# Attention masks: added on VectorE in one fused add and max, and as one strided product per transposed score bank

## The chip, the cores and the metric

The kernel runs on one core of one Trainium2 chip. The metric is the device time of one execution in microseconds (us); the kernel before the change has a median of 1923.84 us over 3 runs (1919.12 to 1926.26). The engines are TensorE (PE, with its weight loads shown apart as PEld), VectorE (DVE), ScalarE (ACT), GpSimd (POOL) and the queue that issues all transfers here, SyncE (SP).

## The reference

One sequence of 2048 rows and 576 columns goes through a sliding-window attention and a mixer with an MLP, each inside an adaptive layer norm. The change touches the attention alone. In short:

```
qkv   = h @ wqkv                       # 32 heads of width 18
scores[h,q,k] = (q . k) * 18**-0.5
mask  = (q - k >= 0) & (q - k < 256)   # each row sees itself and the 255 rows ahead of it
p     = softmax(where(mask, scores, -1e9))
x     = x + ga * ((p @ v) @ wo)
```

Everything else (layer norms, conditioning vector, token mixing, MLP with a GELU) is the same in both kernels.

## The kernel before, in words

The program has four stages, one after the other, with small overlaps: the query/key/value products (to about 228 us of the profile), the attention (to about 735 us), the mixing, and the MLP (from about 1000 us to the end). Each step of a stage is recorded with a due time; the records are sorted by it and written out in that order, so every engine's queue holds its instructions in the order of these times, and nothing is reordered afterwards. The due times of the attention are written as multiples of a head; the change leaves all of them as they are.

The attention goes over 32 units called heads in the code (`n`). A unit holds 512 query rows and two real heads (`j` = 0, 1); units 0 to 7 hold the first 512 rows, where nothing precedes the first row. In each, the scores are computed twice:

- **Row maxima.** Queries stand in blocks of 64 rows. `mx(n, j, bb)` (L440) computes for two blocks a score tile of 128 partitions (64 queries of two real heads) by 320 keys in PSUM, one matmul a block (L448), and then adds the mask with a second matmul, in which the identity is the weight and `Mq` the moving operand (L450, L452). The two PSUM buffers of this tile, `m0` and `m1`, alternate. `red(n, j, bb)` (L454) takes the negated maximum of both blocks in one VectorE reduction (L460), or in two for the narrow blocks of units 0 to 7 (L464). When all eight are there, `mtr` (L466, matmul at L468) transposes the maxima, `mev` copies them on ScalarE, and `mst` sends them by DMA into a row of the query tile, so that the second computation of the scores subtracts them by itself.
- **Transposed scores.** `xm(n, j, k)` (L484) fills five banks of 512 columns with key blocks against query ranges (L492) and adds the masks with one or two identity matmuls a bank (L517). `ex` (L519) takes the exponential of a bank on ScalarE. These banks alternate between `s0` and `s1`.

Every second unit an `av` step (L530) multiplies the exponentials with the values: some 170 to 208 small matmuls in a row on PE. `onm` (L556) normalizes on VectorE. From unit 12 on, every second unit also carries one row tile of the output projection: `otev` (L612) splits the transposed rows, with VectorE at L617 and L618; two runs of 14 matmuls (L629); `woe` (L631) adds each to the residual on VectorE (L633); then come the row statistics (L116 to L118) and the layer norm on VectorE (L642, L643). PE, VectorE and ScalarE each take their instructions strictly in the order of the queue. A buffer is handed on by semaphores: an `mx` matmul cannot start before the reduction two steps earlier has freed its buffer, and `mt` cannot start before the last reduction of its unit.

The loads of a unit are issued on SP behind the maxima of two units earlier.

Of the kernel before, what the change touches and what calls it, by code (L numbers as in the profile page):

```python
# [7 lines left out]
F32 = mybir.dt.float32  # L8
# [3 lines left out]
ALU = mybir.AluOpType  # L12
# [19 lines left out]
class Kern:  # L32
# [8 lines left out]
    def setup(self, stack):  # L41
# [12 lines left out]
        self.rowm = c.tile([P, 8], F32, name="rowm")  # L54
        self.Mq = c.tile([P, 2, 64], F32R, name="Mq")
        self.Mk = c.tile([P, 2, 64], F32R, name="Mk")
        self.md = c.tile([P, 10], F32, name="md")
# [33 lines left out]
    def masks(self):  # L91
        nc = self.nc
        g = nc.gpsimd
        for M in (self.Mq, self.Mk):
            g.memset(M.bitcast(F32), 0.0)
        h = slice(0, 64)
        sel = lambda t, s, op, cm: g.affine_select(out=t, in_=t.bitcast(F32), pattern=[[s, 64]], compare_op=op, fill=NEG, base=0, channel_multiplier=cm)
        sel(self.Mq[h, 0], 1, ALU.is_gt, -1)
        sel(self.Mq[h, 1], -1, ALU.is_ge, 1)
        sel(self.Mk[h, 0], -1, ALU.is_gt, 1)  # L100
        sel(self.Mk[h, 1], 1, ALU.is_ge, -1)
        for M in (self.Mq, self.Mk):
            nc.vector.tensor_copy(M[64:128], M[0:64].bitcast(F32))
        m = self.rowm
# [287 lines left out]
    def attention(self, t1, t2, TA, HU, LX=2.05):  # L392
# [47 lines left out]
        def mx(n, j, bb):  # L440
# [3 lines left out]
            for s in range(2):  # L444
                i = 2 * bb + s
                nb = 5 if g else min(5, i + 1)
                lhs = Q[:, i].rearrange("p r q -> p (r q)")
                nc.tensor.matmul(pm[:, s, 320 - 64 * nb:320], lhs, K[:, j, 64 * (i + 5 - nb):64 * (i + 5)], start=True, stop=False)  # L448
                if nb == 5:
                    nc.tensor.matmul(pm[:, s, 0:320].rearrange("p (a b) -> p a b", b=64)[:, 0::4, :], self.identr, self.Mq, start=False, stop=True)  # L450
                else:
                    nc.tensor.matmul(pm[:, s, 256:320], self.identr, self.Mq[:, 1], start=False, stop=True)  # L452

        def red(n, j, bb):  # L454
# [3 lines left out]
            c = 8 * j + 2 * bb  # L458
            if n >= 8 or bb >= 2:
                nc.vector.tensor_reduce(out=m[:, c:c + 2], in_=pm[:, :, 0:320], axis=mybir.AxisListType.X, op=ALU.max, negate=True)  # L460
# [23 lines left out]
        def xm(n, j, k):  # L484
# [3 lines left out]
            blocks = [x for x in BANKS[k] if g or x[0] >= 0]  # L488
            mk = []
            for i, (b, c) in enumerate(blocks):  # L490
                q0, q1 = rng(b)
                nc.tensor.matmul(px[:, c:c + q1 - q0], K[:, b + 4].rearrange("p r k -> p (r k)"), Q[:, j, q0:q1], start=(i == 0), stop=False)  # L492
                if b >= 0:
                    mk.append((c, 1))
                if b <= 3:
                    mk.append((c + q1 - q0 - 64, 0))
            mk.sort()
            runs = []
            for c, kind in mk:
                if kind == 1 and runs and runs[-1] == (c - 64, 64, 0):  # L500
                    runs[-1] = (c - 64, 128, 0)
                else:
                    runs.append((c, 64, kind))
            if len(runs) == 2 and runs[0][1] == 128 and runs[1][1] == 128:
                d = runs[1][0] - runs[0][0]
                c = runs[0][0]
                out = px[:, c:c + 128]
                o2 = px.rearrange("p (a b) -> p a b", b=64)
                a0, da = c // 64, d // 64
                for h in range(2):  # L510
                    pass
                full = [(o2[:, a0 + h:a0 + h + da + 1:da, :], self.Mk[:, h].unsqueeze(1).to_broadcast([P, 2, 64])) for h in range(2)]
                ops = full
            else:
                ops = [(px[:, c:c + w], self.Mk.rearrange("p a b -> p (a b)")[:, 64 * kind:64 * kind + w]) for c, w, kind in runs]
            for i, (o, mv) in enumerate(ops):
                nc.tensor.matmul(o, self.identr, mv, start=False, stop=(i == len(ops) - 1))  # L517

# [751 lines left out]
```

## Time and profile before

| | |
|---|---|
| median of 3 runs | 1923.84 us (1919.12 to 1926.26) |
| the profiled execution | 1925.45 us, span 1923.7 us |
| mean granted TensorE clock | 0.956 |
| busy, share of the span: PE | 1766.7 us, 92% |
| PEld | 1617.1 us, 84% |
| DVE | 1124.2 us, 58% |
| ACT | 697.9 us, 36% |
| POOL | 899.6 us, 47% |

The page lists, for groups of equal instructions, the line, the engine, the operation, the output and the inputs with their shapes, the count, the busy time, the mean duration in ns, and the idle time just ahead of them with what ended it. A matmul's row gives its duration with the pipeline's length in it; matmuls that follow each other overlap, so a matmul's place in time is read from the distance of two starts. The granted clock is a share of TensorE's full speed.

### The profile page before, as it was taken

What the parts mean: (1) busy time and instruction counts of PE and PEld (TensorE: products, weight loads), DVE (VectorE), ACT (ScalarE), POOL (GpSimd) and SP (SyncE); (2) the same over time, 40 slices, a digit from 0 to 9 for tenths busy, and PEclk for the clock granted to TensorE, in tenths of its full rate; (3) what the DMA queues carried; (4) which work ended last, traced back from release to release, by engine and by line L of the source; (5) the groups of instructions that cost most, each with busy time, mean ns of one, the idle gap of its engine ahead of it and who ended that gap; (6) DMA issues with size and microseconds to landing.
All of it is one profiled execution on the core that took longest, in us unless ns stands there. A gap on an engine that the chain in (4) does not pass through costs nothing.

```text
span 1923.7 us, 34258 instructions
## 1 busy us (share of the span) xinstructions
PE 1766.7 (92%) x13752; PEld 1617.1 (84%) x13752; DVE 1124.2 (58%) x1840; ACT 697.9 (36%) x1194; POOL 899.6 (47%) x831
## 2 busy tenths in 40 slices
PE   7999998989999996787767999999998999999998
PEld 6788888889898986787756999999987899999997
DVE  4544335546665654666646666666676766666664
ACT  2222134434444444423314333333333333333331
POOL 4311364443544444244356556565552555555560
PEclk9999958899999998998887999999998999999999
DMA  4855552443635435444252211121214222222211
GB/s 149 305 178 176 166 144 78 116 123 114 177 110 172 123 93 177 149 154 154 73 175 82 58 58 58 58 58 58 59 56 135 60 58 60 60 61 60 59 46 49
DMA packets 156134, 206.75 MB, mean 107 GB/s; under 512 B 19012, under 2 KB 87620, under 8 KB 155400
## 3 DMA queue, kind: packets, MB, share of 16 engines
q1 hardware_dynamic: 155976, 204.57, 34.6%
q8 instruction: 108, 1.77, 0.4%
q14 instruction: 50, 0.41, 0.1%
HBM read 143.69 MB, written 60.56 MB: 106 GB/s over the span
## 4 chain that ended last, share of the span: by engine, by line
PE 57%; DVE 8%; DMA 3%; POOL 3%; ACT 3%; issue 3%; SPq 1%; DVEq 0%; POOLq 0%; ACTq 0%
PE d L1135 23%; PE av L544 3%; PE wo L629 3%; PE mx L448 2%; PE X L492 2%; PE w L856 2%; PE pg L807 1%; DVE W L994 1%; PE X L517 1%; DVE G L1112 1%; DMA wf<-in_B_w_dram 1%; PE mx L450 1%; PE u33P L1082 1%; PE u32P L1082 1%; PE u26P L1082 1%
## 5 line engine op out<-in xcount | busy, mean ns | idle before, releaser
L1135 PE MATMUL d<-W,G 128*128 128x288 f32 x3456 | 510.2, 298 | 12.5 <-DVE acc L1143 10.0
L1135 PEld LDWEIGHTS d<-W,G 128*128 128x128 f32 x3456 | 490.6, 190 | 35.2 <-DVE acc L1143 10.9
L1143 DVE TENSOR_TENSOR acc<-d,acc 128x576 f32<-128x576 f32 x288 | 216.7, 754 | 193.8 <-PE d L1135 189.5
L974 POOL TENSOR_TENSOR wf<-wf 128x384 f32<-128x384 f32 x140 | 144.9, 1056 | 351.9 <-DMA wf<-in_B_w_dram 351.9
L460 DVE TENSOR_REDUCE m<-mx 128x2 f32<-128x640 f32 x224 | 181.1, 817 | 172.9 <-PE mx L450 171.3
L522 ACT ACTIVATE P<-X 128x512 f32<-128x512 f32 (+4 forms) x320 | 182.0, 573 | 229.1 <-PE X L517 228.0
L448 PE MATMUL mx<-KD,QS 128*128 128x320 f32 (+4 forms) x512 | 168.5, 379 | 28.0 <-POOL QS L431 14.0
L492 PE MATMUL X<-QD,KS 128*128 128x64 f32 (+2 forms) x704 | 156.2, 313 | 1.2 <-ACT P L522 0.7
L431 POOL TENSOR_SCALAR QS<-QD,rowm 128x512 fp32r<-128x512 f32 x128 | 87.8, 699 | 144.0 <-DMA QD<-qd 89.8
L1112 DVE TENSOR_TENSOR G<-U,G 128x512 fp32r<-128x512 f32 x108 | 94.4, 874 | 99.0 <-ACT G L1105 99.0
L986 POOL TENSOR_TENSOR W<-wf,W 128x768 fp32r<-128x768 f32 x70 | 148.8, 2148 | 0.0
L1103 ACT ACTIVATE U<-U 128x512 f32<-128x512 f32 x108 | 68.4, 633 | 189.5 <-DVE U L1088 189.5
L448 PEld LDWEIGHTS mx<-KD,QS 128*128 128x128 f32 x512 | 104.0, 203 | 34.4 <-POOL QS L431 19.3
L1103 ACT ACTIVATE C<-C 128x512 f32<-128x512 f32 x36 | 22.7, 632 | 286.7 <-DVE C L1088 286.7
L278 PE MATMUL qk<-hT,Wqk 128*128 128x512 f32 x504 | 121.3, 402 | 0.0
L278 PEld LDWEIGHTS qk<-hT,Wqk 128*128 128x128 f32 x504 | 96.1, 192 | 24.3 <-issue 0.9
L517 PE MATMUL X<-Mk,identr 128*128 128x128 f32 (+1 forms) x576 | 112.3, 269 | 0.0
L492 PEld LDWEIGHTS X<-QD,KS 128*128 128x128 f32 x704 | 109.1, 199 | 2.5 <-ACT P L522 1.8
L1000 POOL TENSOR_TENSOR wf<-wf,gb 128x1152 f32<-128x1152 f32 x35 | 103.1, 2946 | 13.1 <-DMA wf<-in_B_w_dram 6.9
L438 POOL TENSOR_SCALAR KS<-KD,rowm 128x768 fp32r<-128x768 f32 (+1 forms) x128 | 108.5, 862 | 0.0
L980 ACT CAST W<-wf 128x1152 fp32r<-128x1152 f32 x70 | 90.2, 1319 | 47.2 <-DMA wf<-in_B_w_dram 34.6
L1015 POOL TENSOR_TENSOR W<-wf,W 128x1152 fp32r<-128x1152 f32 x35 | 96.3, 2752 | 13.8 <-ACT W L1009 13.8
(745 smaller groups left out, 3287.2 us busy)
## 6 DMA issues: line engine op xcount, KB each, us to landing
wf<-in_B_w_dram SPq DMA_DIRECT2D x35, 576.0 KB
wf<-in_B_w_dram SPq DMA_DIRECT2D x140, 128.0 KB
KD<-kd SPq DMA_DIRECT2D x72, 216.0 KB
QD<-qd SPq DMA_DIRECT2D x96, 144.0 KB
wf<-in_B_w_dram SPq DMA_DIRECT2D x140, 64.0 KB
qd<-qs SPq DMA_DIRECT2D x16, 512.0 KB
kd<-qs SPq DMA_DIRECT2D x16, 512.0 KB
vd<-Vst SPq DMA_DIRECT2D x16, 312.0 KB
```

What stands on the lines that cost most here:

```text
L278: nc.tensor.matmul(po, W[:, a, fs], H[:, c, :], start=(n == 0), stop=(n == 13))
L438: nc.gpsimd.tensor_scalar(t[:, b0:, r], src[:, b0:], M[:, 2 + r:3 + r], 0.0, op0=ALU.mult, op1=ALU.add)
L448: nc.tensor.matmul(pm[:, s, 320 - 64 * nb:320], lhs, K[:, j, 64 * (i + 5 - nb):64 * (i + 5)], start=True, stop=False)
L460: nc.vector.tensor_reduce(out=m[:, c:c + 2], in_=pm[:, :, 0:320], axis=mybir.AxisListType.X, op=ALU.max, negate=True)
L492: nc.tensor.matmul(px[:, c:c + q1 - q0], K[:, b + 4].rearrange("p r k -> p (r k)"), Q[:, j, q0:q1], start=(i == 0), stop=False)
L517: nc.tensor.matmul(o, self.identr, mv, start=False, stop=(i == len(ops) - 1))
L522: nc.scalar.activation(p[:, lo:], X["px", n, j, k][:, lo:], AF.Exp, scale=SCALE)
L974: nc.gpsimd.tensor_tensor(out=WF[:, o], in0=WF[:, a], in1=WF[:, b], op=ALU.subtract)
L986: eng.tensor_tensor(out=W[:, s0:s1, 3:5, :], in0=WF[:, 1 + s0:1 + s1, 0:2], in1=W[:, s0:s1, 0:2, :].bitcast(F32), op=ALU.subtract)
L1112: nc.vector.tensor_tensor(out=G[:, 1, ta, b], in0=up_b[jj, "gf", ta, b], in1=G[:, 0, ta, b].bitcast(F32), op=ALU.subtract)
L1135: nc.tensor.matmul(po, G[:, g, ta, b, ts], W[:, w, b, cs], start=(n == 0), stop=(n == 5))
L1143: nc.vector.tensor_tensor(out=a, in0=po, in1=a, op=ALU.add)
```

## The change

The mask matmuls of the row maxima go (L450, L452). `Mq` becomes one bf16 row of 320 columns a partition, with the two triangles at both ends and zeros between. `red` issues for each of the two blocks one fused VectorE operation that adds the mask to the scores, writes the sum to a scratch tile `scr` and takes the maximum. The sign that the reduction gave is now given by ScalarE's copy of the transposed maxima, as a multiplication by -1.

In the transposed banks the one or two mask matmuls become one. `Mk` now holds five blocks of 64 columns (two triangles, a zero block, two triangles), and one matmul with 256 moving columns writes to two pieces of 128 columns of the bank, at a stride; where a triangle has no neighbour, the zero block stands beside it. The fifth bank keeps its single matmul.

```diff
-        self.Mq = c.tile([P, 2, 64], F32R, name="Mq")
-        self.Mk = c.tile([P, 2, 64], F32R, name="Mk")
+        self.Mq = c.tile([P, 320], BF16, name="Mq")
+        self.Mk = c.tile([P, 5, 64], F32R, name="Mk")
...
+            X["scr"] = a1([P, 320], F32, name="scr")
...
-                nc.tensor.matmul(pm[:, s, 320 - 64 * nb:320], lhs, K[:, j, 64 * (i + 5 - nb):64 * (i + 5)], start=True, stop=False)
-                if nb == 5:
-                    nc.tensor.matmul(pm[:, s, 0:320].rearrange("p (a b) -> p a b", b=64)[:, 0::4, :], self.identr, self.Mq, start=False, stop=True)
-                else:
-                    nc.tensor.matmul(pm[:, s, 256:320], self.identr, self.Mq[:, 1], start=False, stop=True)
+                nc.tensor.matmul(pm[:, s, 320 - 64 * nb:320], lhs, K[:, j, 64 * (i + 5 - nb):64 * (i + 5)], start=True, stop=True)
...
-            if n >= 8 or bb >= 2:
-                nc.vector.tensor_reduce(out=m[:, c:c + 2], in_=pm[:, :, 0:320], axis=mybir.AxisListType.X, op=ALU.max, negate=True)
-            else:
-                for s in range(2):
-                    w = 64 * (2 * bb + s + 1)
-                    nc.vector.tensor_reduce(out=m[:, c + s:c + s + 1], in_=pm[:, s, 320 - w:320], axis=mybir.AxisListType.X, op=ALU.max, negate=True)
+            for s in range(2):
+                i = 2 * bb + s
+                w = slice(0 if n >= 8 else max(0, 256 - 64 * i), 320)
+                nc.vector.tensor_tensor_reduce(out=X["scr"][:, w], in0=pm[:, s, w], in1=self.Mq[:, w], scale=1.0, scalar=NEG, op0=ALU.add, op1=ALU.max, accum_out=m[:, c + s:c + s + 1])
...
-            nc.scalar.copy(ms, X["mt", n])
+            nc.scalar.mul(ms, X["mt", n], -1.0)
...
+            pairs = lambda c, st: AP(px[:, 0:1].tensor, px[:, c:c + 1].offset, [px[:, 0:1].ap[0], (st, 2), (1, 128)])
+            mk = lambda a, w: self.Mk[:, a:a + w].rearrange("p a b -> p (a b)")
+            split = lambda m: m.rearrange("p (a b) -> p a b", a=2)
+            es = mk(0, 2)
+            both = es.unsqueeze(1).to_broadcast([P, 2, 128])
+            if g:
+                o, mv = ((pairs(0, 256), split(mk(1, 4))), (pairs(128, 256), split(mk(0, 4))), (pairs(0, 320), both), (pairs(64, 320), both), (px[:, 192:320], es))[k]
...
-            for i, (o, mv) in enumerate(ops):
-                nc.tensor.matmul(o, self.identr, mv, start=False, stop=(i == len(ops) - 1))
+            nc.tensor.matmul(o, self.identr, mv, start=False, stop=True)
```

Only PE's and DVE's queues change in what stands in them; SP's, ACT's and POOL's hold the same steps in the same order. The line numbers below are those of each kernel: L448, L492 and L517 of before are L451, L488 and L499 now, and L460 is L461.

PE's queue of before, in unit 18, right behind an `av` step (`mx_0_1` and `mx_0_2` are row-maximum tiles, `X_0_1` and `X_0_2` transposed banks; the shape is that of the output):

```order
L448 MATMUL mx_0_1_5702<-KD_1975,QS_0_5521 128x320
L450 MATMUL mx_0_1_5702<-Mq,identr 128x2x64
L448 MATMUL mx_0_1_5702<-KD_1975,QS_0_5521 128x320
L450 MATMUL mx_0_1_5702<-Mq,identr 128x2x64
L492 MATMUL X_0_1_5709<-QD_1971,KS_0_5497 128x192
L492 MATMUL X_0_1_5709<-QD_1971,KS_0_5497 128x320
L517 MATMUL X_0_1_5709<-Mk,identr 128x128
L517 MATMUL X_0_1_5709<-Mk,identr 128x64
L492 MATMUL X_0_2_5728<-QD_1971,KS_0_5497 128x64
L492 MATMUL X_0_2_5728<-QD_1971,KS_0_5497 128x320
L492 MATMUL X_0_2_5728<-QD_1971,KS_0_5497 128x128
L517 MATMUL X_0_2_5728<-Mk,identr 128x2x64 x2
```

The same place now:

```order
L451 MATMUL mx_0_1_5398<-KD_1976,QS_0_5223 128x320 x2
L488 MATMUL X_0_1_5403<-QD_1972,KS_0_5200 128x192
L488 MATMUL X_0_1_5403<-QD_1972,KS_0_5200 128x320
L499 MATMUL X_0_1_5403<-Mk,identr 128x2x128
L488 MATMUL X_0_2_5422<-QD_1972,KS_0_5200 128x64
L488 MATMUL X_0_2_5422<-QD_1972,KS_0_5200 128x320
L488 MATMUL X_0_2_5422<-QD_1972,KS_0_5200 128x128
L499 MATMUL X_0_2_5422<-Mk,identr 128x2x128
```

Four matmuls a row-maximum tile have become two; the two masks of a bank have become one of 256 columns. Nothing stands in another order.

DVE's queue of before, later in unit 18, with the semaphores that each instruction waits for (PE_49, DVE_49: PE's and DVE's own; `m` holds the maxima):

```order
L460 TENSOR_REDUCE m_5698<-mx_1_0_5769 128x2 [waits PE_49]
L561 RECIPROCAL rc_0_5794<-ot_0_5774 128x16 [waits PE_49]
L562 TENSOR_TENSOR o_5793<-ot_0_5774,rc_0_5794 128x16x18 [waits DMAHW1_49,DVE_49]
L561 RECIPROCAL rc_1_5799<-ot_1_5779 128x16 [waits PE_49]
L562 TENSOR_TENSOR o_5793<-ot_1_5779,rc_1_5799 128x16x18 [waits DVE_49]
L460 TENSOR_REDUCE m_5698<-mx_1_1_5802 128x2 [waits PE_49]
```

The same place now:

```order
L461 ISA scr,m_5393<-mx_1_0_5459,Mq 128x320 [waits DVE_49,PE_49]
L461 ISA m_5393 128x1
L461 ISA scr,m_5393<-mx_1_0_5459,Mq 128x320 [waits DVE_49]
L461 ISA m_5393 128x1
L543 RECIPROCAL rc_0_5482<-ot_0_5462 128x16 [waits PE_49]
L544 TENSOR_TENSOR o_5481<-ot_0_5462,rc_0_5482 128x16x18 [waits DMAHW1_49,DVE_49]
L543 RECIPROCAL rc_1_5487<-ot_1_5467 128x16 [waits PE_49]
L544 TENSOR_TENSOR o_5481<-ot_1_5467,rc_1_5487 128x16x18 [waits DVE_49]
L461 ISA scr,m_5393<-mx_1_1_5490,Mq 128x320 [waits PE_49]
L461 ISA m_5393 128x1
L461 ISA scr,m_5393<-mx_1_1_5490,Mq 128x320 [waits DVE_49]
L461 ISA m_5393 128x1
```

One reduction a tile has become two fused operations, and each of them is two instructions: the operation itself, and one that writes the accumulated maximum to `m`. Since all of them write the one tile `scr`, a fused operation that follows another waits for DVE's own semaphore, that is for the end of the instruction pair ahead of it.

More of the change, by code (lines that the diff above doesn't have):

```diff
@@ L5 @@
 from concourse import mybir
+from concourse.ap import AP
 from concourse.masks import make_identity
@@ L488, in xm @@
             blocks = [x for x in BANKS[k] if g or x[0] >= 0]
-            mk = []
             for i, (b, c) in enumerate(blocks):
@@ L492, in xm @@
                 nc.tensor.matmul(px[:, c:c + q1 - q0], K[:, b + 4].rearrange("p r k -> p (r k)"), Q[:, j, q0:q1], start=(i == 0), stop=False)
[L493 to L513, printed above, removed]
-            else:
-                ops = [(px[:, c:c + w], self.Mk.rearrange("p a b -> p (a b)")[:, 64 * kind:64 * kind + w]) for c, w, kind in runs]
-            for i, (o, mv) in enumerate(ops):
-                nc.tensor.matmul(o, self.identr, mv, start=False, stop=(i == len(ops) - 1))
+            pairs = lambda c, st: AP(px[:, 0:1].tensor, px[:, c:c + 1].offset, [px[:, 0:1].ap[0], (st, 2), (1, 128)])
[5 more added lines that the diff above has]
+                o, mv = ((pairs(0, 256), split(mk(1, 4))), (pairs(128, 256), split(mk(0, 4))), (pairs(0, 320), both), (pairs(64, 320), both), (px[:, 192:320], es))[k]
+            else:
+                sz = split(mk(1, 4))
+                o, mv = ((pairs(0, 256), sz), (pairs(192, 256)[:, :, 0:64], self.Mk[:, 1:4:2]), (pairs(64, 256), sz), (pairs(128, 256), sz), (px[:, 256:320], mk(1, 1)))[k]
+            nc.tensor.matmul(o, self.identr, mv, start=False, stop=True)
         def ex(n, j, k):
```

15 lines of the change are left out of this document (8 added, 7 removed).

## The prediction

> **What bounds the kernel now.** I read the page first, then busy time and clock by stretch, then the timelines of PE and DVE over one period of the attention. From the page and its groups:
>
> ```profile
> L450 PE MATMUL mx<-Mq,identr 128*128 128x128 f32 x448 | 102.2, 228 | 0.0
> L517 PE MATMUL X<-Mk,identr 128*128 128x128 f32 (+1 forms) x576 | 112.3, 269 | 0.0
> L460 DVE TENSOR_REDUCE m<-mx 128x2 f32<-128x640 f32 x224 | 181.1, 817 | 172.9 <-PE mx L450 171.3
> ```
>
> By busy time the masks of the maxima cost PE 102 us and the other masks 112, while the reductions wait 173 us for PE: it looks as if PE alone sets the pace and the masks were worth 150 us. Stretches (span, then PE, PEld, DVE, ACT, POOL busy, granted clock, DMA):
>
> ```profile
> 240.00:282.00 42.00, 38.46 (x173) 37.69 (x174) 18.23 (x40) 13.60 (x28) 29.18 (x33) 0.52 0.52 149
> 282.00:394.00 112.00, 98.64 (x1165) 89.81 (x1163) 53.19 (x97) 47.27 (x97) 43.74 (x62) 0.88 0.39 103
> 394.00:710.00 316.00, 298.71 (x3987) 281.38 (x3986) 187.91 (x320) 143.89 (x269) 140.99 (x207) 0.99 0.46 133
> ```
>
> The stretch that counts is 394 to 710: full clock, PE busy in 95% of it, units 12 to 32. It repeats with every second unit; the chain of waits shows the `av` steps, six periods apart here, so a period is (615.46 - 427.26)/6 = 31.4 us, and the stretch holds ten:
>
> ```profile
> 427.26 4.84 PE av L544 x167
> 615.46 5.18 PE av L544 x182
> ```
>
> One period on PE (start, duration):
>
> ```profile
> 590.54 0.36 PE L448 MATMUL mx<-KD,QS 128*128 128x320 f32 x1
> 590.80 0.36 PE L448 MATMUL mx<-KD,QS 128*128 128x320 f32 x1
> 591.06 0.51 PE L492 MATMUL X<-QD,KS 128*128 128x128 f32 x3
> 591.41 0.41 PE L517 MATMUL X<-Mk,identr 128*128 128x128 f32 x2
> 591.66 0.36 PE L448 MATMUL mx<-KD,QS 128*128 128x320 f32 x1
> 597.49 2.13 PE L629 MATMUL wo<-Wo,T 128*128 128x288 f32 x14 [0.29 <-DVE T L617]
> ```
>
> Starts, not durations, are what PE pays: a maxima matmul with its mask takes 0.26 us together (590.54 to 590.80), not 0.36 + 0.22; a bank of three matmuls and two masks 0.60.
>
> The same period on DVE:
>
> ```profile
> 593.99 0.25 DVE L561 RECIPROCAL rc<-ot 128x16 f32<-128x16 f32 x1
> 595.30 0.81 DVE L460 TENSOR_REDUCE m<-mx 128x2 f32<-128x640 f32 x1
> 596.74 0.69 DVE L617 TENSOR_TENSOR T<-pa,T 128x512 fp32r<-128x512 f32 x1 [0.62 <-ACT T L615]
> 597.55 0.82 DVE L460 TENSOR_REDUCE m<-mx 128x2 f32<-128x640 f32 x1
> 600.72 0.82 DVE L460 TENSOR_REDUCE m<-mx 128x2 f32<-128x640 f32 x1 [2.35 <-PE mx L450]
> 601.46 0.45 DVE L633 TENSOR_TENSOR xr<-wo,xr 128x288 f32<-128x288 f32 x1
> 601.82 0.81 DVE L460 TENSOR_REDUCE m<-mx 128x2 f32<-128x640 f32 x1
> 605.07 0.82 DVE L460 TENSOR_REDUCE m<-mx 128x2 f32<-128x640 f32 x1 [2.43 <-PE mx L450]
> 605.81 0.45 DVE L633 TENSOR_TENSOR xr<-wo,xr 128x288 f32<-128x288 f32 x1
> 606.54 0.44 DVE L117 BATCH_NORM_STATS2 b6st<-xr 128x6 f32<-128x288 f32 x1
> 607.02 0.21 DVE L118 BATCH_NORM_AGGREGATE b6mv<-b6st 128x2 f32<-128x12 f32 x1
> 607.15 1.50 DVE L460 TENSOR_REDUCE m<-mx 128x2 f32<-128x640 f32 x2
> 609.55 1.03 DVE L642 SCALAR_TENSOR_TENSOR h<-xr,b6mv,cb 128x576 f32<-128x576 f32 x1
> 611.42 0.82 DVE L460 TENSOR_REDUCE m<-mx 128x2 f32<-128x640 f32 x1
> 612.16 0.45 DVE L116 BATCH_NORM_STATS2 c6st<-h 128x6 f32<-128x288 f32 x1
> 613.13 2.44 DVE L460 TENSOR_REDUCE m<-mx 128x2 f32<-128x640 f32 x3
> 621.33 0.82 DVE L460 TENSOR_REDUCE m<-mx 128x2 f32<-128x640 f32 x1 [5.77 <-PE mx L450]
> ```
>
> DVE's idle time is no free reserve: it lies in three places, at the two runs of the output projection and at `av`. There PE issues nothing for DVE for a while, and only two score tiles exist ahead.
>
> **The change on PE.** A 288-column matmul of the projection takes 2.13/14 = 0.152 us, so one of 320 about 0.165; without its mask a maxima matmul saves 0.095. In a period of 32 that is 3.0 us. Two banks of five go from five matmuls with 768 columns to four with 768, at a fifth of 0.60 less 0.12 each; two trade a matmul for 64 more columns, 0 to 0.06; the fifth stays. Four sets a period: 1.0 to 1.4, I take 1.2. **PE's own work falls from 31.4 to 27.2 us a period.**
>
> **The change on DVE.** A pair of fused operation and accumulator read, start to next start, is R; a tile costs 2R where it cost 0.74 (600.72 to 601.46). The trace has neither, so R is bounded. The nearest main operation reads one operand from PSUM and one from SBUF:
>
> ```profile
> L633 DVE TENSOR_TENSOR xr<-wo,xr 128x288 f32<-128x288 f32 x32 | 14.2, 446 | 10.2 <-PE wo L629 10.2
> L617 DVE TENSOR_TENSOR T<-pa,T 128x512 fp32r<-128x512 f32 x16 | 11.0, 685 | 10.9 <-ACT T L615 10.9
> L151 DVE MEMSET ct<- 128x5 f32 x1 | 0.1, 62 | 0.0
> L108 DVE TENSOR_TENSOR rowm<-rowm,ident 128x2 f32<-128x2 f32 x1 | 0.2, 161 | 0.0
> ```
>
> From 446 ns at 288 columns and 685 at 512 it is 1.07 ns a column, so 480 ns at 320. An operation that waits for nothing starts 0.09 before the end of the one ahead (601.46 + 0.45 against 601.82); one that waits for DVE's own result starts 0.04 behind it (606.54 + 0.44 against 607.02). The read has no input, as the memset of 62 ns; the smallest operation with inputs takes 161. Low end: no tail and a hidden read, 0.48 - 0.09 + 0.04 = 0.43. High end: the read starts at the end and takes 161 ns, 0.48 + 0.16 + 0.04 = 0.68. I take **R = 0.55**: the read starts in the tail like any next operation, takes 60 to 160 ns and so ends some 0.03 behind the main operation, and the next one waits 0.04 for it.
>
> [...]
>
> **The period on DVE.** Its other work, from the rows: from 593.99 to 595.30 1.31 (`onm`), 0.81 (L617, L618), 0.36, 605.81 to 607.15 1.34, 609.55 to 611.42 1.87, 612.16 to 613.13 0.97: 6.7 us. The three starved stretches: 597.55 to 600.72, 3.17; 601.82 to 605.07, 3.25; and from the end of the second of the three reductions at 613.13, when the last maxima of a unit are there and `mt` can go, 613.13 + 2 x 0.81 = 614.75, to 621.33, 6.6. Sum 13.0, less 0.4 for the masks that PE saves in them: 12.6. Into each fits just one tile. The other 13 of 16 tiles stand outside: before 13 x 0.74 + 6.7 + 13.0 = 29.3 us, under PE's 31.4, so PE set the period. Now **26R + 6.7 + 12.6 = 26R + 19.3**: at R = 0.55 33.6 us, at 0.43 30.5, at 0.68 37.0. Break-even with 31.4 is R = 0.465, less than the main operation alone. What is queued behind the slower pairs: L617 before the first projection run, L633 before `mt` and the second run, the layer norm before the next tiles; PE waits for each, and its saved 4.2 us go into these waits. Ten periods: 10 x (33.6 - 31.4) = +22 us (-9 to +56).
>
> **The first twelve units.** From 240 to 282 the clock is 0.52 and PE is the bound; a unit takes 15.0 us (`mt` to `mt`), and what a mask costs at the low clock shows behind a later pause:
>
> ```profile
> 266.62 0.40 PE L468 MATMUL mt<-ident,m 128*16 128x128 f32 x1
> 281.60 0.40 PE L468 MATMUL mt<-ident,m 128*16 128x128 f32 x1
> 362.56 0.61 PE L448 MATMUL mx<-KD,QS 128*128 128x320 f32 x1 [3.40 <-POOL QS L431]
> 362.96 0.31 PE L450 MATMUL mx<-Mq,identr 128*128 128x128 f32 x1
> 363.07 0.58 PE L448 MATMUL mx<-KD,QS 128*128 128x320 f32 x1
> ```
>
> A mask costs 0.11 there (362.96 to 363.07), 16 a unit 1.8, and with the banks up to 3 us of the 15, over 42/15 = 2.8 units, 8; I let 6 of it arrive, since the next unit's loads come no sooner: -6. From 282 to 394 PE waits for loads (98.6 busy of 112), there is no projection, and I give -1; bounds of both together -15 to +2. Constants, ScalarE's sign and the queues of SP and POOL are the same steps beside waiting engines: 0.
>
> Sum: +22 - 7 = +15 on the profiled execution's 1925.45, 1940.5; that execution stood 1.6 above the median of 1923.84, so **1939 us** (+0.8%).
>
> **The rivals.**
>
> *The fused operation is cheap (faster).* At R = 0.43, from the shortest pitch that rows allow, the period is 30.5: -9, and with -10 from the first units about 1905. If DVE were never late, PE's 27.2 would rule: -42 and -10, 1872. For it: DVE is only 59% busy from 394 to 710. Against it: the self-wait stands in the queue, and its 0.04 is a row. It decides from R below 0.465.
>
> *The clock falls (slower).* Between 240 and 282 PE is busy and the clock stays at 0.52, so a fallen clock does not come back in this mixture. If PE's new waits (up to 2 us) let it fall in the second unit of each period, six steps there cost about 1.8 us (twice 0.40 for a tile, from 362.56 to 362.96, and about 1 for a bank) instead of 2R = 1.1: +4 a period, +40 over the forecast, 1979. Against it: the row at 362.56 shows a fall (0.51 for a masked maxima matmul instead of 0.26) behind a pause of 3.40 us, and none of my waits is so long. The Trainium skill, "TensorE: Matmul & The Clock Gate", section "Part 1: The HAM clock gate (the "warmup" mystery)", puts the limit at about 3.4 us of idleness; the row agrees.
>
> *The accumulator read is slow (slower).* R = 0.68, 37.0 a period: +56 - 5, about 1975.
>
> That the products do not merge is ruled out: PE's queue holds one mask a bank.
>
> **How the numbers follow.** A change of 0.5%, 9.6 us, is about what a measurement can tell: same is 1914 to 1933.5. Forecast, R from 0.48 to 0.60: 0.53, of which 0.20 lies under 1933.5 (R to 0.53); its own range is 1920 to 1955. Cheap operation 0.20, clock 0.13, slow read 0.14. So slower 0.33 + 0.13 + 0.14 = 0.60, same 0.20, faster 0.20. The range leaves out half of the cheap case below and a third of the slow ones above: 1905 to 1977.
>
> **What would show it.** Right: a pair pitch of 0.52 to 0.60 at L461; DVE over 75% busy between the same `av` steps; a period of 33 to 34.5 us; PE waiting for DVE's maxima, 3 to 7 us a period against about 1; the stages ahead and behind unchanged. Wrong: a period under 31, a pitch under 0.465, or a granted clock well under 0.9 from 394 on.

## The result

The changed kernel takes **1951.93 us** (median of 4 runs, 1949.72 to 1954.86) against 1925.05 (4 runs of the kernel before, 1919.12 to 1927.32): a ratio of **1.0145, 95% interval 1.0118 to 1.0173**. It is slower, as forecast and inside the range, but by 27 us where the forecast was 15. The profiled execution took 1954.86 us, span 1953.1.

The three stretches of before, in the profile of the changed kernel (span, then PE, PEld, DVE, ACT, POOL busy, granted clock, DMA):

```profile
240.00:282.00 42.00, 30.06 (x111) 24.27 (x111) 24.59 (x115) 13.03 (x28) 29.78 (x34) 0.57 0.57 159
282.00:394.00 112.00, 87.65 (x1093) 72.98 (x1100) 64.90 (x280) 46.95 (x99) 48.21 (x68) 0.87 0.40 105
394.00:710.00 316.00, 265.77 (x3304) 222.12 (x3289) 199.19 (x741) 134.16 (x251) 133.75 (x195) 0.91 0.45 127
```

From 394 to 710 PE is busy for 266 us instead of 299: its work has gone, and the time has not. The clock is 0.91 there instead of 0.99. That 0.91 is a mean: the clock is full, and falls to half for 3.4 or 6.8 us once in each period, nine times in the stretch. Two of these falls in the changed kernel (the same columns):

```profile
563.40:594.10 30.70, 24.05 (x253) 20.30 (x238) 20.67 (x77) 13.55 (x25) 10.46 (x17) 1.00 0.43 120
594.13:597.52 3.39, 3.39 (x92) 2.50 (x99) 0.83 (x4) 0.86 (x2) 3.39 (x5) 0.50 0.14 36
624.86:631.64 6.78, 5.59 (x108) 4.12 (x114) 3.15 (x14) 1.46 (x3) 5.93 (x9) 0.50 0.58 202
```

The kernel before has no fall from 398.4 to 708.9:

```profile
398.40:708.90 310.50, 293.35 (x3875) 277.14 (x3857) 187.81 (x319) 143.03 (x267) 137.50 (x202) 1.00 0.46 133
```

The groups of the new operations:

```profile
L461 DVE CUSTOM_DVE_ANT_0 scr<-mx,Mq 128x320 f32<-128x320 f32 (+4 forms) x512 | 239.3, 467 | 188.4 <-PE mx L451 160.4
L461 DVE DVE_READ_ACCUMULATOR2_ANT m<- 128x1 f32 x512 | 42.2, 83 | 0.0
```

Where the saved work went is in the waits of PE. Before, from 394 to 710 (us in total, times, longest):

```profile
PE mt L468 <- DVE xr L633: 4.2, 10, 0.4
PE mx L448 <- DVE m L460: 4.0, 11, 0.6
PE wo L629 <- DVE T L617: 2.1, 7, 0.3
PE mt L468 <- DVE m L460: 1.3, 1, 1.3
```

After, the same stretch:

```profile
PE mx L451 <- DVE m L461: 14.2, 18, 1.5
PE mt L465 <- DVE xr L615: 7.7, 9, 0.9
PE mt L465 <- DVE m L461: 3.0, 9, 0.6
PE wo L611 <- DVE T L599: 2.9, 7, 0.4
```

The `av` steps in the chain of waits of the changed kernel (start, duration):

```profile
424.70 5.63 PE av L526 x201
730.82 6.15 PE av L526 x200
756.39 5.12 PE av L526 x183
```

Nine periods take 730.82 - 424.70 = 306.1 us, 34.0 each; the kernel before has 31.46 (427.26 to 710.39). And the period on DVE after the change:

```profile
567.84 0.49 DVE L461 CUSTOM_DVE_ANT_0 scr<-mx,Mq 128x320 f32<-128x320 f32 x1 [8.07 <-PE mx L451]
568.25 0.08 DVE L461 DVE_READ_ACCUMULATOR2_ANT m<- 128x1 f32 x1
568.37 0.49 DVE L461 CUSTOM_DVE_ANT_0 scr<-mx,Mq 128x320 f32<-128x320 f32 x1
569.01 0.49 DVE L461 CUSTOM_DVE_ANT_0 scr<-mx,Mq 128x320 f32<-128x320 f32 x1
575.37 0.48 DVE L461 CUSTOM_DVE_ANT_0 scr<-mx,Mq 128x320 f32<-128x320 f32 x1
578.27 0.49 DVE L461 CUSTOM_DVE_ANT_0 scr<-mx,Mq 128x320 f32<-128x320 f32 x1 [1.87 <-PE mx L451]
579.22 0.45 DVE L615 TENSOR_TENSOR xr<-wo,xr 128x288 f32<-128x288 f32 x1
579.59 0.48 DVE L461 CUSTOM_DVE_ANT_0 scr<-mx,Mq 128x320 f32<-128x320 f32 x1
582.56 0.49 DVE L461 CUSTOM_DVE_ANT_0 scr<-mx,Mq 128x320 f32<-128x320 f32 x1 [1.95 <-PE mx L451]
593.97 0.49 DVE L461 CUSTOM_DVE_ANT_0 scr<-mx,Mq 128x320 f32<-128x320 f32 x1
601.27 0.49 DVE L461 CUSTOM_DVE_ANT_0 scr<-mx,Mq 128x320 f32<-128x320 f32 x1 [6.27 <-PE mx L451]
```

The main operation takes 0.49 us. Its read starts 0.08 before it ends and ends with it. The second operation of a tile starts 0.53 behind the first (567.84 to 568.37), the first one of the next tile 0.64 behind that (to 569.01): 1.17 a tile where tiles follow each other. A tile behind which another kind of operation stands takes 0.95 (578.27 to 579.22).

### The profile page after: what moved, and what is told of

The parts are those of the page before. It is cut to its first block, busy times and chain, and to the rows that moved or that the text cites. A ratio compares the mean times of both kernels' runs of the same rounds, so it can differ in the third digit from the quotient of the medians.

```text
span 1953.1 us, 33645 instructions
## 1 busy us (share of the span) xinstructions
PE 1737.5 (89%) x12984; PEld 1546.2 (79%) x12984; DVE 1163.2 (60%) x2577; ACT 696.7 (36%) x1194; POOL 898.9 (46%) x831
## 4 chain that ended last, share of the span: by engine, by line
PE 54%; DVE 12%; POOL 3%; ACT 3%; issue 3%; DMA 2%; SPq 1%; DVEq 0%; POOLq 0%; ACTq 0%
PE d L1117 23%; DVE scr L461 4%; PE av L526 3%; PE wo L611 2%; PE pg L789 2%; PE w L838 2%; DVE W L976 1%; PE X L488 1%; DMA wf<-in_B_w_dram 1%; PE mx L451 1%; DMA rows<-xmd 1%; PE u25P L1064 1%; PE u32P L1064 1%; PE u30P L1064 1%; PE u9P L1064 1%
## 5 line engine op out<-in xcount | busy, mean ns | idle before, releaser
L461 DVE CUSTOM_DVE_ANT_0 scr<-mx,Mq 128x320 f32<-128x320 f32 (+4 forms) x512 | 239.3, 467 | 188.4 <-PE mx L451 160.4
L451 PE MATMUL mx<-KD,QS 128*128 128x320 f32 (+4 forms) x512 | 135.2, 349 | 66.5 <-DVE m L461 23.1
L488 PE MATMUL X<-QD,KS 128*128 128x64 f32 (+2 forms) x704 | 150.3, 306 | 5.4 <-ACT P L504 5.0
L451 PEld LDWEIGHTS mx<-KD,QS 128*128 128x128 f32 x512 | 86.0, 208 | 82.2 <-DVE m L461 29.4
L488 PEld LDWEIGHTS X<-QD,KS 128*128 128x128 f32 x704 | 115.9, 202 | 19.7 <-ACT P L504 17.3
L1085 ACT ACTIVATE C<-C 128x512 f32<-128x512 f32 x36 | 22.7, 632 | 283.6 <-DVE C L1070 283.6
L982 POOL TENSOR_TENSOR wf<-wf,gb 128x1152 f32<-128x1152 f32 x35 | 102.6, 2933 | 13.2 <-DMA wf<-in_B_w_dram 6.9
L499 PE MATMUL X<-Mk,identr 128*128 128x256 f32 (+2 forms) x320 | 100.8, 315 | 0.0
```

The lines of the kernel that those rows point to most:

```text
L461: nc.vector.tensor_tensor_reduce(out=X["scr"][:, w], in0=pm[:, s, w], in1=self.Mq[:, w], scale=1.0, scalar=NEG, op0=ALU.add, op1=ALU.max, ...
L499: nc.tensor.matmul(o, self.identr, mv, start=False, stop=True)
L982: nc.gpsimd.tensor_tensor(out=R4, in0=R4, in1=gb.unsqueeze(1).to_broadcast([P, 2, D]), op=ALU.mult)
```

## The experiments

Two theories stood against each other at the start. **Theory 1**: DVE's pairs, one behind the other, set the period. **Theory 2**: the lower clock that comes with PE's waits makes a large part of the loss. Theory 3 was that the strided product itself gains nothing. All runs in one view; "period" is the mean of nine, from the sixth `av` step to the fifteenth, "step" the mean time from the first product of an `av` step to the next product on PE over those ten steps, "clock" the granted clock from 394 to 710, all of each kernel's first profile. Ratios are to the runs of the kernel before on the same chips (medians 1923.5 to 1925.9).

| kernel | median us | ratio to before (95%) | period | step | clock |
|---|---|---|---|---|---|
| before | 1925.05 | | 31.46 | 5.14 | 0.99 |
| the change | 1951.93 | 1.0145 (1.0118 to 1.0173) | 34.01 | 6.41 | 0.91 |
| bank masks alone | 1912.2 | 0.9932 (0.9904 to 0.996) | 30.74 | 4.81 | 0.99 |
| fused maxima alone | 1956.25 | 1.0156 (1.0122 to 1.019) | 34.64 | 6.52 | 0.91 |
| change, two scratch tiles | 1920.86 | 0.9962 (0.9936 to 0.9988) | 31.96 | 6.16 | 0.94 |
| change, one bf16 scratch tile | 1955.11 | 1.0157 (1.0121 to 1.0192) | 33.99 | 6.43 | 0.90 |
| change, zero products | 1957.72 | 1.0162 (1.0131 to 1.0193) | 33.88 | 5.73 | 0.95 |
| two scratch tiles, zero products | 1927.29 | 1.0012 (0.9998 to 1.0026) | 31.59 | 5.09 | 0.99 |
| half of the tiles fused | 1919.2 | 0.9976 (0.9959 to 0.9993) | 31.19 | 5.03 | 0.99 |
| fused in the first units only | 1919.99 | 0.998 (0.9963 to 0.9996) | 31.29 | 5.30 | 0.99 |
| before, tiles placed as after | 1929.74 | 1.0029 (1.0012 to 1.0047) | 31.40 | 5.12 | 0.99 |

### The two parts apart

The bank masks alone, on the kernel before:

```diff
-            mk = []
-            ... (one or two products, built from runs of blocks)
+            pairs = lambda c, st: AP(px[:, 0:1].tensor, px[:, c:c + 1].offset, [px[:, 0:1].ap[0], (st, 2), (1, 128)])
+            ... (the table of the change)
+            nc.tensor.matmul(o, self.identr, mv, start=False, stop=True)
```

> The kernel before with one part of the change alone: one strided mask product for each transposed bank; the maxima keep their masks on PE and their one reduction for two blocks. Theory 1 (the accounting of the prediction: before, PE sets the period; the banks take 1.2 us of its 31.4 away, and the loss of the whole change comes from VectorE's pairs alone): 1.0 to 1.4 us a period, 10 to 14 us over ten, 2 to 4 more in the first units, so 12 us faster than before (10 to 17), about 1912 where before stands at 1925; the period between the av steps of the stretch 394 to 710 about 30.2. Rival 3 (the strided product is as slow as the two that it replaces, or PE gives the time back in waits): within 3 us of before, or slower, the period 31.2 or more.

Measured: 1912.2 us, 13 faster than before. The period is 30.74 (0.7 less, where 1.2 was expected), and the first units end earlier (sixth `av` step at 419.8 against 427.2). Theory 3 falls: the strided product pays. The shares differ from the working, since part of each period's gain goes into waits even here: PE waits 9.2 us for DVE's maxima in the nine periods, against 3.7 before.

The fused maxima alone, with the bank masks as before:

```diff
-                nc.tensor.matmul(pm[:, s, 320 - 64 * nb:320], lhs, ..., start=True, stop=False)
-                ... (mask product)
+                nc.tensor.matmul(pm[:, s, 320 - 64 * nb:320], lhs, ..., start=True, stop=True)
...
+                nc.vector.tensor_tensor_reduce(out=X["scr"][:, w], in0=pm[:, s, w], in1=self.Mq[:, w], ...)
```

> The other part alone: fused add and max on VectorE, transposed banks masked as before, in two products where there were two. Theory 1 (VectorE's pairs, two for each tile, set the period now, and PE's saving goes into waits): PE's own work in a period is 28.4 instead of 27.2 and still far under 34, so the time is that of the full change, within 0 to +5 us of it (1950 to 1958, +1.3 to +1.7% on before). If PE still sets much of the end in the changed kernel, the 1.2 us a period come back in full: +10 to +15 on the full change, 1962 to 1967.

Measured: 1956.25 us, 4 above the full change and 31 above before. So the change joins a part that gains 13 us with one that costs 31. And the gain of the banks shrinks from 13 us to some 4 once the maxima are fused, which the two intervals do not separate from nothing: PE's work is hardly what the end waits for any more.

### What the pairs wait for

Two scratch tiles in turn:

```diff
-            X["scr"] = a1([P, 320], F32, name="scr")
+            X["scr"] = [a1([P, 320], BF16, name=f"scr{i}") for i in range(2)]
...
-                nc.vector.tensor_tensor_reduce(out=X["scr"][:, w], ...)
+                nc.vector.tensor_tensor_reduce(out=X["scr"][s][:, w], ...)
```

> The full change, but the sums that nobody reads go into two scratch tiles in turn (type bf16 for want of space, where the change has one of f32), so that a fused operation waits for the pair two before it and no longer for the pair just before. Theory 1 (the pitch of the pairs sets the period with slope 26): if the next operation then starts about 0.09 before the end of the one ahead as the operations do that wait for nothing, the pitch falls from 0.53 to about 0.47 inside a tile, 1 to 2 us a period, and the time falls by 10 to 18 us, to 1934 to 1942. Rival 2 (the fallen clock makes most of the loss) expects a change only by the clock: within 4 us of the full change as long as the clock stays at 0.91. If the pitch doesn't move, the self-wait costs nothing, and the time is that of the full change.

Measured: 1920.86 us, 31 less than the full change, and below the kernel before. The timeline of DVE in this kernel:

```profile
567.27 0.49 DVE L461 CUSTOM_DVE_ANT_0 scr<-mx,Mq 128x320 bf16<-128x320 f32 x1
567.68 0.08 DVE L461 DVE_READ_ACCUMULATOR2_ANT m<- 128x1 f32 x1
567.68 0.49 DVE L461 CUSTOM_DVE_ANT_0 scr<-mx,Mq 128x320 bf16<-128x320 f32 x1
568.10 0.49 DVE L461 CUSTOM_DVE_ANT_0 scr<-mx,Mq 128x320 bf16<-128x320 f32 x1
```

The pitch is 0.41 to 0.42, inside a tile as from one tile to the next: each operation starts 0.08 before the one ahead ends, together with its read. The operation itself is as long as before, 0.49. A tile costs 0.82 instead of up to 1.17, nearly what the single reduction cost (0.74). The gain is larger than the expectation's 10 to 18 us: the period loses 2.05, the upper end of it, and the first units, which the expectation left out, end at 415.2 instead of 424.6.

That it is the wait and not the narrower type is shown by one bf16 tile:

```diff
-            X["scr"] = a1([P, 320], F32, name="scr")
+            X["scr"] = a1([P, 320], BF16, name="scr")
```

> The full change with its one scratch tile in bf16 instead of f32. It keeps the wait of each fused operation for the pair just before it. If the two tiles in turn were so much faster because of that wait, this kernel has the pitch of 0.53 and 0.64 and the time of the full change, 1948 to 1956. If it was the narrower type of the scratch writes, the pitch is 0.41 here too and the time about 1921.

Measured: 1955.11 us, a period of 33.99, and on DVE the old pitches, 0.54 and 0.64:

```profile
571.33 0.49 DVE L461 CUSTOM_DVE_ANT_0 scr<-mx,Mq 128x320 bf16<-128x320 f32 x1 [7.55 <-PE mx L451]
571.87 0.49 DVE L461 CUSTOM_DVE_ANT_0 scr<-mx,Mq 128x320 bf16<-128x320 f32 x1
572.51 0.49 DVE L461 CUSTOM_DVE_ANT_0 scr<-mx,Mq 128x320 bf16<-128x320 f32 x1
```

So what makes the fused maxima dear is that each of them writes sums that nobody reads to the tile that the one ahead wrote. That wait costs 0.12 us a pair, and 0.23 where the operation also waits for a new tile from PE; why the second wait adds to the first was not shown.

### What the clock costs

With the pitch at 0.41, the prediction's 26R + 19.3 gives 30.0 us a period; the kernel with two scratch tiles has 31.96. Its `av` steps are long, and waits for DVE stand ahead of them (of the next one here, which starts at 575.8):

```profile
542.73 6.99 PE L526 MATMUL av<-P,V 64*32 64x320 f32 x208
567.91 0.53 PE L451 MATMUL mx<-KD,QS 128*128 128x320 f32 x2 [0.69 <-DVE m L461]
572.14 0.56 PE L451 MATMUL mx<-KD,QS 128*128 128x320 f32 x2 [1.09 <-DVE m L461]
```

The same 208 products (every `av` step of the stretch has as many; the chain of waits lists fewer) took 5.14 us before in the mean of ten steps, and 4.74 at best. Two kernels keep PE busy with products of zeros in the place of the masks, one on the full change and one on two scratch tiles:

```diff
-                nc.tensor.matmul(pm[:, s, 320 - 64 * nb:320], lhs, ..., start=True, stop=True)
+                nc.tensor.matmul(pm[:, s, 320 - 64 * nb:320], lhs, ..., start=True, stop=False)
+                zero = self.Mk[:, 2]
+                if nb == 5:
+                    nc.tensor.matmul(pm[:, s, 0:320]...[:, 0::4, :], self.identr, zero.unsqueeze(1).to_broadcast([P, 2, 64]), start=False, stop=True)
+                else:
+                    nc.tensor.matmul(pm[:, s, 256:320], self.identr, zero, start=False, stop=True)
```

> The full change, and on PE a product with a block of zeros wherever the kernel before had a mask of the maxima: PE is as busy as without the fused operation, and VectorE does the same as in the full change. It adds work that changes no value. Theory 1 (VectorE's pairs set the period): PE's own work is 30.2 us a period, under 34, so nearly nothing: +2 to +10 us on the full change (the starved stretches get 0.4 us a period longer, the first units lose 2 to 4 us), with the clock at 0.91 or a little higher. Rival 2 (PE's idle time lets the clock fall to 0.91, and this is a large part of the loss): the clock from 394 on comes back to 0.97 or more, the av step from 6.1 to about 5 us, and the time falls by 5 to 12 us.

Measured on the full change: 1957.72 us, 6 more. From 394 to 710:

```profile
394.00:710.00 316.00, 281.43 (x3686) 254.23 (x3686) 197.19 (x733) 132.18 (x249) 134.99 (x195) 0.95 0.45 128
```

By the prediction's price of a mask, PE has 3.0 us more to do in a period, and the period is 33.88 instead of 34.01: PE's sum does not set it, as theory 1 has it. In the `av` step 0.7 us come back; the expectation had 0.4 us of zeros in the starved stretches against them. The intervals of the two ratios overlap, so the 6 us are not clear of noise, and they are not in the profiled execution, which took 1952.99 us. Its first units are longer, 145.9 us from the first to the sixth `av` step, where the three profiles of the change have 140.7 to 143.7.

> Two scratch tiles in turn, and on PE a product with a block of zeros wherever the kernel before had a mask of the maxima; it adds work that changes no value. Theory 2 (with the pairs at a pitch of 0.41, what keeps the period at 32.0 is the clock that falls in the av step, 6.2 us there against 5.1 before): the busier PE keeps its clock at 0.98 or more from 394 to 710, the av step falls to about 5 us, the period to about 31, and the time falls below that of two tiles in turn although PE has more to do: by 5 to 12 us, to 1909 to 1916. Theory 1 alone (the order of VectorE and PE's own work set the period): PE's own 30.2 us fill its waits; 0 to +8 us, 1921 to 1929.

Measured: the clock is back at 0.99, the `av` step at 5.09, and the period at 31.59 instead of 31.96, with some 3.0 us more work on PE. That is theory 2's mechanism, but the period falls by 0.37 where about 1 was expected. The time is 1927.29, 6 more and not 5 to 12 less, and here the intervals lie apart. In the profiles it is the first units that are longer: from the first to the sixth `av` step 141.8 us instead of 135.3. So the fall of the clock is real and costs about 1.1 us in each `av` step (6.16 against 5.09), but keeping the clock up by more work buys almost nothing, and 31.6 instead of 30.0 at full clock says that PE and DVE wait for each other in turns: neither one's sum is the period. What the clock alone costs, without the added work, no run shows. In the full change the `av` step's 1.27 us (6.41 against 5.14) stand in DVE's longest wait of the period, so as an estimate about half of the period's growth of 2.55 us is the clock's.

### Mixing the parts

Fused operations (two scratch tiles) for all tiles of the first twelve units and for every second one of the later units; and the same for the first twelve units alone. The other tiles have their mask from PE, as a bf16 product:

```diff
+        def fused(n, bb):
+            return n < 12 or bb % 2 == 0        # the second kernel: return n < 12
...
+                if not f:
+                    nc.tensor.matmul(pm[:, s, 0:320]...[:, 0::4, :], self.identb, self.Mq...[:, 0::4, :], start=False, stop=True)
```

> A version that takes the parts that paid: the strided bank masks; two scratch tiles in turn; fused operations for every tile of the first twelve units, and for every second tile of the later ones (there the other tiles keep the mask on PE, as a bf16 product, and one reduction for two blocks). From the two runs before: the banks alone end the first units 7.4 us earlier than before and the period at 30.74; two tiles in turn end them 12.0 us earlier. PE's own work is 28.7 us a period and VectorE's order gives 29.5 (eight of its tiles at 0.82, the rest at 0.74): a period of 29.5 to 30.7, so 12 us from the first units and 8 to 19 from ten periods: 1894 to 1905. If the waits between the two make the clock fall as in the full change, the period is 31 or more and the time 1908 or more.

> The strided bank masks for all units; fused operations with two scratch tiles in turn only in the first twelve units, where PE waits for loads and later work anyway; from unit 12 on the mask of the maxima stays on PE (as a bf16 product) with one reduction for two blocks. From the first av step to the sixth the run with the banks alone took 139.8 us and the runs with two scratch tiles in turn 135.3 and 134.8 (before: 144.5); the banks alone make a period of 30.74. If both parts add up: 4.5 to 5 us less than the banks alone, 1905 to 1909. If the first units only end earlier to wait later, 1910 to 1914.

Measured: 1919.2 and 1919.99 us. The first units do end early (sixth `av` step at 418.1 and 417.4, against 419.8 with the banks alone), but the periods are 31.19 and 31.29, longer than the 30.74 of the banks alone, and what lies behind the attention is some 4 us longer. The forecasts of a gain missed. The first kernel's other branch (a period of 31 or more, 1908 us or more) has the numbers and not the reason, since the clock stays at 0.99. Of all versions the bank masks alone have the lowest median, though the interval of two scratch tiles overlaps theirs. With half of the tiles fused, PE waits 24 us for DVE in the nine periods, against 11 before: what PE no longer has to do goes into waits again. Why the last kernel, which does after unit 12 what the banks alone do, has 31.29 was not isolated; its `av` step is 0.5 longer, and its masks are bf16 products.

### What lies behind the attention

The first pair of profiles has 7.6 us of the loss behind the last `av` step, where the code is the same. Further profiles of both kernels:

> The full change once more, to see which parts of its +29.4 us of span come again. The part up to the last av step (21.8 us) should come again within 2 us. The part behind it (mixing and MLP, 7.6 us) should be 0 to 3 in this execution if it was the scatter of single executions, and 5 to 8 again if the change itself makes it.

> The full change a third time: by scatter alone the part behind the attention comes anywhere from 1189 to 1197; if the change lengthens it, 1191 to 1197. Up to the last av step 754 to 757 us, as in its two profiles before.

> The kernel before once more, for the length of what lies behind the attention (from the last av step to the end of the span): 1189.2 us in its first profile, 1196.8 and 1190.8 in the two profiles of the full change. If the change does nothing there and single executions scatter, this kernel shows values between 1189 and 1197 as well. If the change makes that part 2 to 7 us longer, this kernel stays at 1187 to 1191.

> As the run just before: the part behind the attention of the kernel before, between 1189 and 1197 by scatter alone, at 1187 to 1191 if the change lengthens it.

Measured (us of the profiles; single times 1927.88 and 1928.67 for the kernel before, 1948.97 for the third of the change, median 1952.46 of two for the second):

| profile | sixth `av` step | from there to the last | from there to the end | span |
|---|---|---|---|---|
| before, 1 | 427.2 | 307.3 | 1189.2 | 1923.7 |
| before, 2 | 430.4 | 308.2 | 1187.5 | 1926.1 |
| before, 3 | 430.5 | 308.2 | 1188.2 | 1926.9 |
| change, 1 | 424.6 | 331.7 | 1196.8 | 1953.1 |
| change, 2 | 423.2 | 330.8 | 1190.8 | 1944.8 |
| change, 3 | 425.6 | 329.4 | 1192.2 | 1947.2 |
| difference of the means | -4.9 | +22.7 | +5.0 | +22.8 |

The change does lengthen the part behind the attention, by some 5 us. It is in the MLP loop: from its first to its last down product 896.1, 893.4 and 891.7 us before, 900.1, 898.9 and 897.6 after; the third of the change and the last two of before ran on one chip. The down products of before, of the change and of the next experiment (count, ns min/median/max, first and last start):

```profile
L1135 PE MATMUL d<-W,G x3456: 288/294/609, 1023.4 to 1919.5; 128*128 128x288 f32 x192
```

```profile
L1117 PE MATMUL d<-W,G x3456: 290/295/606, 1048.8 to 1948.9; 128*128 128x288 f32 x192
```

```profile
L1136 PE MATMUL d<-W,G x3456: 288/295/610, 1027.4 to 1925.7; 128*128 128x288 f32 x192
```

The median product takes 295 ns instead of 294. What the change alters for this loop is only where tiles lie in memory: its constants are 896 bytes a partition larger, and the attention has one more tile. The kernel before with just that:

```diff
-        self.Mq = c.tile([P, 2, 64], F32R, name="Mq")
-        self.Mk = c.tile([P, 2, 64], F32R, name="Mk")
+        self.Mq = c.tile([P, 160], F32R, name="Mq")[:, 0:128].rearrange("p (a b) -> p a b", a=2)
+        self.Mk = c.tile([P, 5, 64], F32R, name="Mk")[:, 0:2]
...
+            X["scr"] = a1([P, 320], F32, name="scr")
```

> The kernel before with its two mask tiles enlarged to the size they have in the changed kernel (640 and 1280 bytes a partition instead of 512 and 512, the rest unused) and with an unused scratch tile of 320 f32 columns in the attention: nothing else is moved. If the place of the tiles in memory lengthens the MLP loop, its first to last product take 896.6 us or more and the part behind the attention 1191 to 1196, the whole 1927 to 1932. If it is something about the fused operations, the loop takes 891 to 896 and the time is that of the kernel before, 1922 to 1928.

> The same kernel as the run just before, for a second profile: MLP loop of 896.6 us or more if the place of the tiles makes it, 891 to 896 if not.

Measured: 1929.74 us (ratio 1.0029, 1.0012 to 1.0047; the second profile's single time is 1939.48), the MLP loop 898.3 and 899.3 us, the part behind the attention 1194.8 and 1197.9, the median down product 295 ns. So the place of the tiles makes it, without any fused operation. Which tile it is that lies worse was not looked for; the kernel with the banks alone, whose `Mk` is larger but whose `Mq` is not and which has no scratch tile, keeps 894.7 us and 294 ns.

## Why the prediction was right or wrong

**The bound and the sign: right.** PE's work left the period, and DVE's order took its place. PE's four kinds of waits for DVE in the stretch add up to 27.8 us, where they came to 11.6. Adding work back to PE hardly changed the period (33.88), shortening DVE's pairs did (31.96). One thing was taken too simply: the 31.4 us a period that the prediction books as PE's own work hold waits for DVE already, 11.6 us in ten periods, so neither engine's sum was the period before the change either.

**The pitch R: right in size, with the parts put together otherwise.** 0.55 was taken; inside a tile it is 0.53. The read is hidden (the low bound's assumption). That bound took 0.09 for a tail off as well; by the prediction's own rows a hidden read alone gives 0.48 + 0.04 = 0.52 and not 0.43. The next operation starts 0.04 behind the end of the one ahead, as worked out. What no row of before showed is the 0.64 where the operation waits for its own engine and for PE together. The prediction priced the self-wait at 0.13 a pair in passing (from 0.09 ahead to 0.04 behind) and it is 0.12; but it was treated as a given, and it is the one thing that decides the sign of the whole: without it the pitch is 0.41, under the break-even of 0.465 that the prediction named, and the time is under that of the kernel before.

**The period: right, in part by luck.** 26R + 19.3 gave 33.6; it is 34.0. From 567.84 to 601.27, 33.43 us, the starved stretches are 578.27 - 575.37 = 2.90, 582.56 - 579.59 = 2.97 and 601.27 - 593.97 = 7.30, together 13.2 against 12.6. The remaining 20.3 us are the thirteen tiles and the other work, for which the prediction had 14.3 and 6.7. Two errors cancel: tiles with another operation behind them are cheaper (0.95), and `av` is slower at the fallen clock, which the sum had at nothing. This period has one of the short falls and an `av` step of 5.86; with the mean of 6.41 it is the 34.0. From the sixth to the last `av` step: +22 forecast, +22.7 measured in the means of three profiles.

**The clock: a rival that came true, at a lower price.** It was set aside because none of PE's waits would be as long as the 3.40 us of its row. They are not: the longest in the stretch is 1.5 us; still the clock falls once in each period, as the rival said, and the `av` step grew by 1.27 us. Ahead of the fall at 594.13 stand several waits of PE within 5 us:

```profile
590.83 0.56 PE L451 MATMUL mx<-KD,QS 128*128 128x320 f32 x2 [1.40 <-DVE m L461]
592.74 0.53 PE L451 MATMUL mx<-KD,QS 128*128 128x320 f32 x2 [1.06 <-POOL c5rs L121]
593.88 0.28 PE L465 MATMUL mt<-ident,m 128*16 128x128 f32 x1 [0.60 <-DVE m L461]
```

The rule that stood beside that argument, some 3.4 us of idleness (the Trainium skill, "TensorE: Matmul & The Clock Gate", section "Part 1: The HAM clock gate (the "warmup" mystery)"), was no bound here: the clock fell with no single wait above 1.5 us. The price of that rival, +4 a period on top of the forecast, was too high. Which rule the clock follows was not settled.

**The rest of the program, put at 0: wrong.** This is the step that failed: constants and the other queues were "the same steps beside waiting engines: 0", and the stages behind were to stay unchanged. The part behind the attention is 5.0 us longer, and the run with tiles placed as after shows 6 us (+0.29%) from the place of the tiles alone. The prediction went by the instructions, which are the same in the later stages, and did not ask what the larger constants move in memory.

**The first twelve units, -7: too large a gain.** The means give -4.9, inside the bounds. This is the second term of the sum that was mis-sized, and its failed step is that PE alone bounds these units. PE's waits from 240 to 394 for loads that come by POOL (`QS`) and for DVE's maxima, of before, of the change, and, for the maxima, with two scratch tiles:

```profile
PE mx L448 <- POOL QS L431: 12.3, 4, 3.4
PE mt L468 <- DVE m L460: 0.9, 4, 0.3
```

```profile
PE mx L451 <- POOL QS L434: 19.0, 7, 4.5
PE mx L451 <- DVE m L461: 7.3, 18, 1.0
PE mt L465 <- DVE m L461: 3.6, 6, 0.7
```

```profile
PE mx L451 <- DVE m L461: 3.5, 11, 0.5
PE mt L465 <- DVE m L461: 1.7, 5, 0.5
```

Of PE's saved work some 7 us more went into waiting for `QS` (while one wait of 3.6 us for another load is gone), which the prediction allowed for when it let only a part of the saving arrive, and 10 us into waiting for the maxima, which it did not see.

Of the 12 us between forecast and medians, the term of the rest makes 5.0, the first units 2.1, the periods 0.7. The remaining 4 lie between the medians (+27) and the means of the profiled executions (+22.8, which is the low end of the interval); nothing in the traces accounts for them. In the first pair of profiles, from which the forecast of 1940.5 was made, nothing is left over: of the 14.4 us up to 1954.86 the rest makes 7.6, the first units 4.4 (-2.6 instead of -7) and the periods 2.4.

**The rivals.** *The fused operation is cheap*: not in this kernel. With the self-wait gone it is cheap, but the period was then 31.96 and not 30.5, so the price of that rival was wrong as well: it took one engine's order for the period. *The accumulator read is slow*: no, 0.08 us and hidden. The Trainium skill, "VectorE: DVE Perf Modes", section "The DRAIN you can't avoid", says that a semaphore behind each operation costs nothing extra; here the runs with one and with two scratch tiles differ by 0.12 us a pair and 31 us in all, and the measurement decides.

**The signs named ahead.** Pitch 0.52 to 0.60: 0.53, and 0.64 at a new tile. Period 33 to 34.5: yes. PE's waits: for DVE's maxima, which the sign named, 17.2 us in the 9.3 periods of the stretch, 1.9 a period and so under 3 to 7; with its waits for DVE's other results 27.8, or 3.0. DVE over 75% busy: wrong, 63% (199.19 of 316): the pairs overlap with their reads and the self-waits count as idle, so the busy share hid the bound once more. Stages behind unchanged: wrong. A clock well under 0.9 would have spoken against the forecast; it is 0.91.

## What to carry to other kernels

An operation whose full output nobody reads still waits for the tile that it writes: give such outputs two tiles in turn before judging the operation by its pitch. Where two engines wait for each other in turns, take neither one's sum as the new period, and count a busier engine's relief only as far as the other one's order lets it through. When a change resizes tiles that live through the whole program, compare the stages that it does not touch too: a profile of each kernel three times is enough to see 5 us in 1900.

## What the runs showed of the hardware

- A fused add and max over 320 columns from PSUM takes 0.49 us on VectorE; its accumulator read (81 to 86 ns) starts 0.08 before its end and adds nothing. Back to back the pair costs 0.41 us, 0.53 with a wait for the engine's own result, 0.64 with a second wait for PE.
- PE's granted clock fell to half for 3.4 or 6.8 us once in each period (0.91 in the mean instead of 0.99), though its longest wait in the stretch was 1.5 us. With products of zeros added the mean was 0.95 and 0.99.
- Constants 896 bytes a partition larger, with one more tile in an earlier stage, made an unchanged MLP loop of 894 us some 5 us longer: the median of its 3456 down products went from 294 to 295 ns.
